# Group 4's attention output turned by the DMA crossbar instead of TensorE, and the block that reads it begun by halves of 256 tokens

## The chip, the core and the metric

The kernel runs on one core of one Trainium2 chip. The time is the device time of that core in microseconds (us). A core has five engines that work side by side, each through its own instructions in its own order: TensorE (PE in the profile) multiplies matrices, and its weight loads are shown apart as PEld; VectorE (DVE), ScalarE (ACT) and GpSimd (POOL) work element by element; SyncE (SP) does nothing here but issue DMA transfers. An engine whose next instruction waits does not go on to the one behind it.

## The reference

Two layers follow each other. The first is attention in which a query sees the first 4 keys ("sinks") and the 128 latest ones; there are 4 batches, 8 heads, 768 positions and a head size of 64. The second is a feed-forward block on the 3072 tokens of 512 features that come out of it.

```python
scores = scale * np.matmul(q, k.transpose(0, 1, 3, 2))
keep = (pos[None, :] < n_sink) | ((rel >= 0) & (rel < window))
a = softmax(np.where(keep, scores, -1e9))
x = np.matmul(a, v).transpose(0, 2, 1, 3).reshape(B * S, H * D)
g, val = x @ w_gate, x @ w_val          # 512 -> 1536, twice
out = (g * sigmoid(g) * val) @ w_out    # 1536 -> 512
```

## The kernel before, in words

**Groups and blocks.** The attention works on 12 groups of 256 tokens, three to a batch (groups 0 to 2 are batch 0, and so on; `c` is a group's place in its batch). The feed-forward works on blocks of tokens: blocks 0, 1 and 2 have 256 tokens each (groups 0, 1, 2), blocks 3 to 6 have 512 (groups 3 and 4, 5 and 6, 7 and 8, 9 and 10), and block 7 has 256 (group 11).

**The steps of a group.** From group 4 on, a group goes through these:
- `NV(g)`: GpSimd issues four loads of k and q into the tile `nat` (line 111) and two of v into `va` (line 122). All groups from 4 on share one buffer for `nat`, so the loads of group g+1 wait until group g's `nat` has been read.
- `xbar(g)`: SP issues four DMA transposes from `nat` to kT and qT (line 255), in the order k, q of the first 128 tokens, k, q of the last 128. "The crossbar" is this kind of DMA.
- `step_S(g, 0)` and `(g, 1)`: the scores of heads 0 to 3 and 4 to 7 (matmuls of line 288), ScalarE's exponential (295), VectorE's mask (300). `step_K` does the sinks' scores (line 316).
- `step_PV(g, j, hh)`: probabilities times v for 128 tokens j and half of the heads hh (lines 331 and 351), then VectorE's reciprocal and product into `xn` (359, 365). A group has four, in the order hh 0 with j 0 and 1, then hh 1 with j 0 and 1.
- `step_X(g, j)`: turns `xn` of 128 tokens into `xT`, features on the partitions. For groups in the list `PEX` this is four TensorE transposes (line 392) and a VectorE copy (line 399); for the others SP issues one DMA transpose (line 387). It is called X(g, j) below.

**The feed-forward.** A gate unit computes 512 columns: four matmuls of 512 columns for the gate (tile `pg`, line 413), ScalarE's tanh (433), four matmuls for the value (`pv`), and two VectorE instructions that make `ht` (441, then 447 or 443). For a block of 256 tokens one unit takes two of the twelve slices of 128 features, in eight matmuls of 256 columns each. A down unit computes 128 tokens of the output in twelve matmuls (`pd`, line 488), a ScalarE copy (493) and a DMA to the output (496).

**The order.** It is written out by hand: `manual_schedule` keeps it as the program issues it. `weave` runs a list of units and puts the attention's steps into them: into a gate unit between the gate's and the value's matmuls, into a down unit evenly between its twelve matmuls. The first weave has 24 units, 0 to 23; units 18 to 23 are the down units of blocks 0, 1 and 2, and it holds the steps of groups 2, 3 and 4 and the first loads of 5, 6 and 7. The second weave has the twelve gate units and four down units of block 3 and holds groups 5 and 6; scores of group 6 (`step_S(6, 0)`) stand in its unit 6. The third does the same for block 4 and groups 7 and 8, the fourth for block 5 and groups 9 and 10.

Three orders matter around the change. SP issues xbar(5), the output of unit 19, X(3, 0), X(3, 1), the outputs of units 20, 21 and 22, xbar(6), the output of unit 23, xbar(7), X(5, 0), X(5, 1). GpSimd issues NV(5), then `behind(3, 255)`, NV(6), NV(7), `behind(4, 511)`, NV(8). `behind(tb, t)` (line 521) copies one element of column t of xT of block tb, so it holds GpSimd, and with it the loads behind it, until that column has been turned. TensorE does the score matmuls of group 6 when it comes to them; nothing behind them passes them.

PSUM tiles all come from one pool of eight banks that are used in turn, so a step can wait for the reader of the tile eight allocations back.

Of the kernel before, what the change touches and what calls it, by code (L numbers as in the profile page):

```python
# [10 lines left out]
ALU = mybir.AluOpType  # L11
# [3 lines left out]
def kernel(  # L15
# [12 lines left out]
    nc = tc.nc  # L28
# [13 lines left out]
    SIZES = [256, 256, 256, 512, 512, 512, 512, 256]  # L42
    assert sum(SIZES) == NTOK and NG == 12
    OFF = [sum(SIZES[:i]) for i in range(len(SIZES))]
    PEX = (0, 1, 2, 4)

    VS = 72
    FCH = [2] * 6
# [29 lines left out]
    def bank(shape, dtype, name):  # L78
        return psum.tile(shape, dtype, tag="b", name=name)
# [123 lines left out]
    kTs, qTs, es_t, e_t, xns, xTs = {}, {}, {}, {}, {}, {}  # L203
# [168 lines left out]
    def dense(t, c, n):  # L372
        return t[:, 0:c * n].rearrange("p (c n) -> p c n", c=c)

    def step_X(g, j, evict="v"):
        t0 = g * 256 + j * P
        tb = max(i for i in range(len(SIZES)) if OFF[i] <= t0)
        off = t0 - OFF[tb]
        if tb == 0 and off == 0:
            xTs["01"] = xtp.tile([P, DMC, 512], BF16, tag="xT", name="xT")  # L380
            xTs[0], xTs[1] = (xTs["01"][:, :, 256 * i:256 * (i + 1)] for i in range(2))
        elif tb > 1 and off == 0:
            xTs[tb] = dense(xtp.tile([P, DMC * 512], BF16, tag="xT", name="xT"),
                            DMC, SIZES[tb])
        if g not in PEX:
            def sp():
                nc.sync.dma_start_transpose(xTs[tb][:, :, off:off + P], xns[g, j])
            later.append(sp)
            return
        pt = bank([P, DMC, P], BF16, "px")  # L390
        for i in range(DMC):
            nc.tensor.transpose(pt[:, i], xns[g, j][:, i * P:(i + 1) * P], ident)  # L392

        if evict == "a":
            nc.scalar.copy(out=xTs[tb][:, :, off:off + P], in_=pt)
            return

        def dve():
            nc.vector.tensor_copy(out=xTs[tb][:, :, off:off + P], in_=pt)
        if evict == "now":  # L400
            dve()
        else:
            later.append(dve)

    hts = {}

    def project(ws, tb, f, name):
        n = xTs[tb].shape[2]
        ps = bank([P, 512], FP32, name)
        for i in range(512 // n):  # L410
            fi, fo = FOF[f + i]
            for c in range(DMC):
                nc.tensor.matmul(  # L413
                    ps[:, i * n:(i + 1) * n], ws[fi][:, c, fo * P:(fo + 1) * P],
                    xTs[tb][:, c], start=(c == 0), stop=(c == DMC - 1))
        return ps

    def gate_a(tb, f):
        new_h(tb)
        return tanh(project(wgs, tb, f, "pg"))  # L420

    def new_h(tb):
        if tb not in hts:
            n = SIZES[tb]
            t = hpool.tile([P, DFC * 512], BF16, tag="ht", name="ht")
            hts[tb] = dense(t, DFC, n)
            if tb == 0:
                hts["01"] = t.rearrange("p (b c n) -> p b c n", b=2, c=DFC)
                hts[1] = t[:, DFC * n:2 * DFC * n].rearrange("p (c n) -> p c n", c=DFC)

    def tanh(pg):
        th = tpool.tile([P, 512], FP32, tag="th", name="th")
        nc.scalar.activation(th, pg, AF.Tanh, scale=0.5)  # L433
        return pg, th

    def gate_b(tb, f, pg, th):
        gate_v(tb, f, pg, th, project(wvs, tb, f, "pv"))

    def gate_v(tb, f, pg, th, pv):
        u = upool.tile([P, 512], BF16, tag="u", name="u")  # L440
        nc.vector.scalar_tensor_tensor(u, th, 1.0, pg, op0=ALU.add, op1=ALU.mult)  # L441
        if tb == "01":
            nc.vector.tensor_tensor(
                hts[tb][:, :, f], *(x.rearrange("p (b n) -> p b n", b=2) for x in (u, pv)),
                op=ALU.mult)
            return
        nc.vector.tensor_tensor(  # L447
            hts[tb][:, f:f + 512 // SIZES[tb]].rearrange("p a n -> p (a n)"), u, pv,
            op=ALU.mult)

    def gate(tb, f, attn):
        a = gate_a(tb, f)
        for step in attn:
            step()
        gate_b(tb, f, *a)
        flush()
# [3 lines left out]
    def gate_held(tb, f, attn):  # L460

        held.append(A(gate_v, tb, f, *gate_a(tb, f), project(wvs, tb, f, "pv")))

    def gate_first(tb, f, attn):

        for j, hh, norm in ((0, 0, "a"), (1, 0, "v"), (0, 1, "v"), (1, 1, "a")):
            step_PV(1, j, hh, norm)
            flush()
        a = gate_a(tb, f)
        step_X(1, 0, "now")  # L470
        step_X(1, 1, "now")
        held.pop()()
        gate_b(tb, f, *a)
# [24 lines left out]
    def gates(tb):  # L498
        return [(gate, tb, f) for f in range(0, DFC, 512 // SIZES[tb])]

    def downs(tb):
        return [(down, tb, t) for t in range(SIZES[tb] // P)]

    def A(fn, *a):
        return lambda: fn(*a)
# [4 lines left out]
    def Ss(g):  # L510
        return [A(step_S, g, p2) for p2 in range(2)]

    def PVs(g):
        return [A(step_PV, g, j, hh) for hh in range(2) for j in range(2)]

    def Xs(g):
        return [A(step_X, g, j) for j in range(2)]
# [5 lines left out]
    def K(g):  # L523
        return A(step_K, g)

    def weave(us, slots):
        assert all(i < len(us) for i in slots)
        for i, (fn, tb, x) in enumerate(us):
            fn(tb, x, slots.get(i, []))

    def slots(*pairs):
        sl = {}
        for at, steps in pairs:
            for i, step in zip(at if isinstance(at, tuple) else (at,) * len(steps),
                               steps):
                sl.setdefault(i, []).append(step)
        return sl
# [114 lines left out]
    def L(*fs):  # L652
        def f():
            for x in fs:
                x()
        return f

    def NV(g):
        return L(A(load_nat, g), A(load_v, g))
# [7 lines left out]
        (15, [A(xbar, 4)]), (15, [NV(5)]), (19, [A(xbar, 5)]),  # L667
        (23, [A(xbar, 6)]), (23, [NV(7)]),
        ((17, 18), Ss(3)), (18, [A(step_ks, 1)]), (18, [A(step_vsb, 1)]),
        ((19, 19, 19, 20), PVs(3)), (20, [*Xs(3), flush, A(behind, 3, 255), NV(6)]),  # L670
        (19, [L(Ss(4)[0], K(4))]), (20, Ss(4)[1:]),
        ((21, 21, 22, 22), PVs(4)), (22, Xs(4))))

    def pair(ga, gb, sh=0):
        s = sh
        return [((s, s + 2), Ss(ga)), (s, [K(ga)]),
                ((s + 4, s + 5, s + 6, s + 7), PVs(ga)),
                ((s + 6, s + 8), Ss(gb)), ((s + 8, s + 9), Xs(ga)), (s + 6, [K(gb)]),
                ((12, 12, 13, 13) if s else (10, 10, 11, 12), PVs(gb)),
                ((14, 14) if s else (12, 13), Xs(gb))]  # L680

    weave(gates(3) + downs(3), slots(
        (2, [A(xbar, 7)]), (15, [A(step_ks, 2), A(step_vsb, 2)]), *pair(5, 6),
        (13, [flush, A(behind, 4, 511), NV(8)]),
        (15, [A(xbar, 8)]), (15, [NV(9)])))
# [43 lines left out]
```

## Time and profile before

| | |
|---|---|
| median of 7 runs | 238.46 us (237.86 to 238.8) |
| profiled execution, its own time | 238.63 us |
| span of the profile | 236.9 us |
| granted TensorE clock, mean | 0.999 |
| busy: TensorE, VectorE, ScalarE, GpSimd | 97%, 67%, 48%, 32% of the span |
| first weave's down units | 55.2 to 75.3 us on TensorE |
| block 3's gate units | 75.3 to 100.6 us |

The page's first part gives the busy time of each engine, and its fourth part follows the chain of work that ended last. The timeline lists an engine's instructions with their start and length in us, equal neighbours merged; SPq rows are the moments at which SP issues a DMA, POOL rows of kind DMA_DIRECT2D those in which GpSimd writes a load's descriptors. A bracket at the end of a row tells how long the engine had been idle and what ended that. The trace also records when each DMA's completion reached its semaphore.

### The profile page before, as it was taken

What the parts mean: (1) busy time and instruction counts of PE and PEld (TensorE: products, weight loads), DVE (VectorE), ACT (ScalarE), POOL (GpSimd) and SP (SyncE); (2) the same over time, 40 slices, a digit from 0 to 9 for tenths busy, and PEclk for the clock granted to TensorE, in tenths of its full rate; (3) what the DMA queues carried; (4) which work ended last, traced back from release to release, by engine and by line L of the source; (5) the groups of instructions that cost most, each with busy time, mean ns of one, the idle gap of its engine ahead of it and who ended that gap; (6) DMA issues with size and microseconds to landing.
All of it is one profiled execution on the core that took longest, in us unless ns stands there. A gap on an engine that the chain in (4) does not pass through costs nothing.

```text
span 236.9 us, 4855 instructions
## 1 busy us (share of the span) xinstructions
PE 228.9 (97%) x1858; PEld 125.8 (53%) x1885; DVE 158.8 (67%) x335; ACT 113.5 (48%) x235; POOL 74.7 (32%) x99
## 2 busy tenths in 40 slices
PE   8899999999999999999999999999999999999994
PEld 4568645795554444544445444444544445488443
DVE  5897888768652888950898980698970598877000
ACT  4794485467453836412846522655622653333221
POOL 8996865713505344005353440080000000000000
PEclk9999999999999999999999999999999999999999
DMA  8999999994999999927989996599314100200132
GB/s 133 160 184 177 181 200 205 160 146 76 157 176 180 127 133 131 118 49 152 150 123 136 119 142 159 134 86 118 66 24 144 56 3 0 44 3 0 55 124 91
DMA packets 107655, 27.36 MB, mean 116 GB/s; under 512 B 94704, under 2 KB 104688, under 8 KB 107632
## 3 DMA queue, kind: packets, MB, share of 16 engines
q0 software_dynamic: 76640, 13.90, 77.2%
q1 hardware_dynamic: 30448, 12.89, 27.4%
q8 instruction: 15, 0.25, 0.4%
q10 hardware_dynamic: 544, 0.26, 0.4%
q14 instruction: 8, 0.07, 0.1%
HBM read 28.34 MB, written 6.29 MB: 146 GB/s over the span
## 4 chain that ended last, share of the span: by engine, by line
PE 89%; DVE 2%; DMA 2%; POOL 2%; issue 2%; ACT 1%; POOLq 0%; DVEq 0%; ACTq 0%
PE pv L413 26%; PE pd L488 26%; PE pg L413 25%; PE s L288 4%; PE o L351 4%; DMA rows<-in_q_dram 2%; DVE xn L365 1%; PE o L331 1%; PE pn L241 1%; POOL rows L100 1%; POOL x L186 1%; PE pk L316 1%; ACT th L433 1%; PE px L392 1%; DVE rcp L359 0%
## 5 line engine op out<-in xcount | busy, mean ns | idle before, releaser
L441 DVE SCALAR_TENSOR_TENSOR u<-th,pg 128x512 bf16<-128x512 f32 x72 | 49.2, 683 | 38.2 <-ACT th L433 38.2
L413 PE MATMUL pg<-xT,wg 128*128 128x512 bf16 (+1 forms) x345 | 73.4, 340 | 0.7
L433 ACT ACTIVATE th<-pg 128x512 f32<-128x512 f32 x72 | 43.4, 603 | 62.9 <-PE pg L413 59.2
L413 PE MATMUL pv<-xT,wv 128*128 128x512 bf16 (+1 forms) x341 | 72.8, 339 | 0.6 <-ACT e L295 0.2
L488 PE MATMUL pd<-wo,ht 128*128 128x512 bf16 (+2 forms) x291 | 64.7, 370 | 0.6 <-issue 0.2
L447 DVE TENSOR_TENSOR ht<-u,pv 128x512 bf16<-128x512 bf16 x64 | 44.0, 688 | 9.6 <-PE pv L413 2.9
L413 PEld LDWEIGHTS <-wg 128*128 128x128 bf16 x352 | 34.3, 98 | 28.4 <-issue 0.4
L295 ACT ACTIVATE e<-s 128x512 bf16<-128x512 f32 (+1 forms) x88 | 42.8, 579 | 3.9 <-PE s L288 3.7
L488 PEld LDWEIGHTS <-ht 128*128 128x128 bf16 x300 | 27.8, 98 | 29.9 <-issue 0.3
L413 PEld LDWEIGHTS <-wv 128*128 128x128 bf16 x352 | 31.4, 98 | 20.9 <-issue 1.7
L493 ACT ACTIVATE ot<-pd 128x512 f32<-128x512 f32 (+1 forms) x24 | 14.3, 596 | 47.2 <-PE pd L488 43.2
L111 POOL DMA_DIRECT2D nat<-in_k_dram x20 | 17.7, 888 | 47.5 <-DMA qT<-nat 43.8
L300 DVE TENSOR_TENSOR e<-e,mask 128x1024 bf16<-128x1024 bf16 (+1 forms) x44 | 27.0, 650 | 3.8 <-ACT e L295 3.8
L122 POOL DMA_DIRECT2D va<-in_v_dram x24 | 21.5, 921 | 4.2 <-DMA wo<-in_moe_w_out_dram 2.5
L365 DVE TENSOR_TENSOR xn<-o,rcp 128x256 bf16<-128x256 f32 x44 | 18.7, 425 | 1.5
L351 PEld LDWEIGHTS <-e 128*128 128x128 bf16 x352 | 15.0, 98 | 7.8 <-issue 0.2
L111 POOL DMA_DIRECT2D nat<-in_q_dram x20 | 17.7, 899 | 1.2 <-DMA wv<-in_moe_w_val_dram 0.5
L351 PE MATMUL o<-va,e 128*128 128x65 bf16 x352 | 17.0, 194 | 0.1
L288 PE MATMUL s<-qT,kT 64*128 64x128 bf16 (+1 forms) x240 | 12.9, 237 | 0.0
L288 PEld LDWEIGHTS <-kT 64*128 64x128 bf16 x240 | 7.7, 94 | 7.5 <-issue 6.6
L495 DVE TENSOR_SCALAR ot<-pd 128x128 f32<-128x128 f32 x1 | 0.3, 292 | 14.3 <-PE pd L488 14.3
L359 DVE RECIPROCAL rcp<-o 128x4 f32<-128x4 f32 x48 | 8.4, 176 | 1.2 <-PE o L351 1.1
(72 smaller groups left out, 93.2 us busy)
## 6 DMA issues: line engine op xcount, KB each, us to landing
out_dram<-ot SPq DMA_DIRECT2D x23, 256.0 KB
va<-in_v_dram POOLq DMA_DIRECT2D x24, 128.0 KB, 6.5
nat<-in_k_dram POOLq DMA_DIRECT2D x20, 128.0 KB, 4.1
nat<-in_q_dram POOLq DMA_DIRECT2D x20, 128.0 KB, 5.9
wg<-in_moe_w_gate_dram POOLq DMA_DIRECT2D x6, 256.0 KB, 8.0
wv<-in_moe_w_val_dram POOLq DMA_DIRECT2D x6, 256.0 KB, 8.3
wo<-in_moe_w_out_dram POOLq DMA_DIRECT2D x4, 384.0 KB, 11.2
st<-in_q_dram ACTq DMA_DIRECT2D x2, 128.0 KB
```

What stands on the lines that cost most here:

```text
L111: nc.gpsimd.dma_start(x[:, i, j].rearrange("p (h d) -> p h d", d=D), src[b, :, t0:t0 + P].rearrange("h p d -> p h d"))
L122: nc.gpsimd.dma_start(va[:, j, :, 0:D], v[b, :, t0:t0 + P].rearrange("h p d -> p h d"))
L288: nc.tensor.matmul(pss[2 * pp + h][:, col:col + n], kTs[b][r, p, kk:kk + P], qTs[b][r, p, qq:qq + n], start=True, stop=True)
L295: nc.scalar.activation(e_t[g][:, h0 + h, lo:512], pss[2 * pp + h][:, lo:512], AF.Exp, scale=scale)
L300: nc.vector.tensor_tensor(e, e, m[:, :, lo:512].broadcast_to([P, 2, 512 - lo]), op=ALU.mult)
L351: nc.tensor.matmul(o, l, r, start=(c == 0 and i == 0), stop=(i == len(mms) - 1), skip_group_check=True)
L365: nc.vector.tensor_tensor(xn, po[:, :, 0:D], rcp.broadcast_to([P, 4, D]), op=ALU.mult)
L413: nc.tensor.matmul(ps[:, i * n:(i + 1) * n], ws[fi][:, c, fo * P:(fo + 1) * P], xTs[tb][:, c], start=(c == 0), stop=(c == DMC - 1))
L433: nc.scalar.activation(th, pg, AF.Tanh, scale=0.5)
L441: nc.vector.scalar_tensor_tensor(u, th, 1.0, pg, op0=ALU.add, op1=ALU.mult)
L447: nc.vector.tensor_tensor(hts[tb][:, f:f + 512 // SIZES[tb]].rearrange("p a n -> p (a n)"), u, pv, op=ALU.mult)
L488: nc.tensor.matmul(po, hts[tb][:, f, ts * P:(ts + 1) * P], wos[f // n][:, f % n, lo:hi], start=(f == 0), stop=(f == DFC - 1))
```

## The change

Group 4 leaves `PEX`, so X(4, 0) and X(4, 1) become DMA transposes on SP. The first two gate units of block 3, which took feature slices 0 and 1 over all 512 tokens, become one unit for slices 0 and 1 of the first 256 tokens (group 3) and one for the same slices of the last 256 (group 4). The second of them alone, of the two, needs group 4. In the first weave the steps of units 20 to 22 are redistributed: X(4, 0) goes to unit 21 behind the third of group 4's four PV steps, X(4, 1) to unit 22 behind the fourth. `behind` and NV(6) move from unit 20 to unit 22, and `behind` now waits for column 511 of block 3's xT, that is for X(4, 1), where it waited for column 255.

SP's order becomes: xbar(5), output 19, X(3, 0), X(3, 1), output 20, X(4, 0), output 21, X(4, 1), output 22, xbar(6), output 23, and on as before.

```diff
-    PEX = (0, 1, 2, 4)
+    PEX = (0, 1, 2)
...
+            if tb == 3:
+                for i in range(2):
+                    xTs[tb, i] = xTs[tb][:, :, 256 * i:256 * (i + 1)]
...
     def gate_a(tb, f):
-        new_h(tb)
+        new_h(tb[0] if isinstance(tb, tuple) else tb)
...
+        if isinstance(tb, tuple):
+            nc.vector.tensor_tensor(
+                hts[tb[0]][:, f:f + 2, 256 * tb[1]:256 * (tb[1] + 1)],
+                *(x.rearrange("p (a n) -> p a n", a=2) for x in (u, pv)), op=ALU.mult)
+            return
...
-        ((19, 19, 19, 20), PVs(3)), (20, [*Xs(3), flush, A(behind, 3, 255), NV(6)]),
+        ((19, 19, 19, 20), PVs(3)), (20, Xs(3)),
         (19, [L(Ss(4)[0], K(4))]), (20, Ss(4)[1:]),
-        ((21, 21, 22, 22), PVs(4)), (22, Xs(4))))
+        ((21, 21, 21, 22), PVs(4)), (21, Xs(4)[:1]),
+        (22, [Xs(4)[1], flush, A(behind, 3, 511), NV(6)])))
...
-    weave(gates(3) + downs(3), slots(
+    weave([(gate, (3, i), 0) for i in range(2)] + gates(3)[2:] + downs(3), slots(
```

## The prediction

> **What bounds the kernel now.** I read the page first, for the engine that is never idle, then the timelines of TensorE, SP and GpSimd around units 20 to 30, which the change touches.
>
> ```profile
> span 236.9 us, 4855 instructions
> ...
> PE 228.9 (97%) x1858; PEld 125.8 (53%) x1885; DVE 158.8 (67%) x335; ACT 113.5 (48%) x235; POOL 74.7 (32%) x99
> ...
> PE 89%; DVE 2%; DMA 2%; POOL 2%; issue 2%; ACT 1%; POOLq 0%; DVEq 0%; ACTq 0%
> ```
>
> TensorE is busy 97% of the span and makes 89% of the chain that ended last: matmul time that goes is won, and a stall of TensorE is lost. Its timeline, where group 4 is turned and where group 6's scores come:
>
> ```profile
> 71.14 0.39 PE L392 MATMUL px<-ident,xn 128*128 128x128 bf16 x4
> 71.36 0.59 PE L488 MATMUL pd<-wo,ht 128*128 128x512 bf16 x2
> 71.80 0.39 PE L392 MATMUL px<-ident,xn 128*128 128x128 bf16 x4
> 72.02 3.40 PE L488 MATMUL pd<-wo,ht 128*128 128x512 bf16 x14
> 75.26 1.03 PE L413 MATMUL pg<-xT,wg 128*128 128x512 bf16 x4
> ...
> 89.17 0.50 PE L288 MATMUL s<-qT,kT 64*128 64x256 bf16 x8
> 89.78 1.04 PE L413 MATMUL pv<-xT,wv 128*128 128x512 bf16 x4
> ```
>
> From start to start, four transposes take 71.14 to 71.36, 0.22 us; block 3 begins at 75.26; group 6's scores at 89.17. SP's queue, then GpSimd's:
>
> ```profile
> 69.75 1.22 SPq L387 DMA_TRANSPOSE xT<-xn  x1
> 71.06 2.81 SPq L496 DMA_DIRECT2D out_dram<-ot  x3
> 77.21 1.19 SPq L255 DMA_TRANSPOSE kT<-nat  x1
> 79.65 1.19 SPq L255 DMA_TRANSPOSE qT<-nat  x1
> 80.94 1.22 SPq L255 DMA_TRANSPOSE kT<-nat  x1
> 82.54 1.19 SPq L255 DMA_TRANSPOSE qT<-nat  x1
> ...
> 105.22 0.49 SPq L496 DMA_DIRECT2D out_dram<-ot  x1
> 105.82 1.23 SPq L387 DMA_TRANSPOSE xT<-xn  x1
> ```
>
> ```profile
> 72.96 0.18 POOL L521 CAST warmed<-xT 1x1 f32<-1x1 bf16 x1 [10.65 <-DMA xT<-xn]
> 73.73 1.77 POOL L111 DMA_DIRECT2D nat<-in_k_dram  x2 [0.60 <-issue]
> ...
> 86.05 1.76 POOL L111 DMA_DIRECT2D nat<-in_k_dram  x2 [7.04 <-DMA qT<-nat]
> ...
> 108.35 0.17 POOL L521 CAST warmed<-xT 1x1 f32<-1x1 bf16 x1 [17.04 <-DMA xT<-xn]
> ```
>
> GpSimd waits for X(3, 1), issued at 69.75, until 72.96; starts group 6's loads at 73.73; and at 86.05 has seen group 6 turned. So group 6 is ready 3.1 us ahead of its scores. That margin is what the change spends.
>
> **Part 1: eight transposes leave TensorE.** 8 x 0.055 (0.22 / 4) = 0.44 us, on the path: matmuls stand right before and after them. VectorE's two copies of xT, 0.42 us each, end at 72.65, and VectorE then sits idle 4.23 us for block 3's first tanh: worth nothing.
>
> **Part 2: halves.** Units 24 and 25 have eight matmuls of 256 columns where four of 512 stood, in four places. The chain has both forms: eight of 256 in block 7 take 0.87 us, four of 512 take 0.86. Cost 4 x 0.01 = 0.04 us. ScalarE's tanh is the same 128x512; VectorE's strided product (line 443) takes 688 ns, as does the plain one (447). Sum so far: -0.44 + 0.04 = -0.40 us.
>
> **Part 3: PV steps move up.** Group 4's third PV moves from unit 22 (69.58) to unit 21, about 68.1. It needs the last mask of step_S(4, 1), which VectorE ends at 67.27 + 0.69 = 67.96; that score step moves up by one matmul (0.22), so about 67.74. Cover 0.1 to 0.35 us, price nothing; without the cover at most 0.2.
>
> **Part 4: two transposes on SP.** An output takes 0.6 us of SP to the next issue (105.22 to 105.82; up to 0.8 behind a transpose), a transpose 1.31 (69.75 to 71.06). So output 20 at 71.06, X(4, 0) about 71.8, output 21 at 73.1 (was 71.86), X(4, 1) at 73.7, output 22 at 75.0 (was 73.54). Both xn are ready earlier, 69.6 and 70.8 by the PV times and 0.6 us of VectorE a step. The outputs delay nobody: ot has four buffers, and the next output tile after unit 23 is written at 103.59. xbar(6), queued behind, waits for data until 77.21 even in the old order. X(4, 1) in the new order follows a transpose and an output, as X(6, 1) did: issued 105.82, GpSimd released 108.35, 2.53 us. By X(3, 1) it is 3.21. So X(4, 1) is there at 76.2, at worst 76.9. Unit 24 starts at 74.82 and needs only X(3), there at 72.96. Unit 24 took 2.61 us (75.26 to 77.86) and takes 2.63, so unit 25 starts at 77.4. Cover 0.5 to 1.2 us, price nothing.
>
> **Part 5: the loads held.** This adds the wait that matters. Behind GpSimd's `behind` are NV(6), NV(7) and `behind(4, 511)`; for NV(6) wait xbar(6) on SP, the scores of group 6 on TensorE, and NV(7). From the release to the first load 0.77 us (72.96 to 73.73), 1.06 in the other case (108.35 to 109.41). So the loads start at 77.0, bounds 76.9 and 78.0, instead of 73.73. From the first load to group 6 turned and seen by GpSimd: 73.73 to 86.05, 12.32; group 8 the same way 11.87 (109.41 to 121.28), group 9 12.50 (121.28 to 133.78). In the trace's completion records the last q transpose landed at 85.49, so GpSimd's step adds 0.56 and landing takes 11.76; by the same records groups 5 and 7 take 12.08 and 11.83, and group 11, the far row, 13.62. I take group 6's own 11.76, since its loads meet the same neighbours (output 22 at the start, its own four transposes): 77.0 + 11.76 = 88.75. Ends: 76.9 + 11.31 (group 8) = 88.2, and 78.0 + 13.62 = 91.6.
>
> Need: 89.17 - 0.40 = 88.77. There is a little more: the pv matmuls behind the scores wait at 89.78 for a PSUM bank that VectorE's xn (89.30, 0.42 long) frees, while the scores are done at 89.61. That chain (tanh at 87.06, u, ht, reciprocal, xn) moves with TensorE, so scores that start up to 0.17 late, 88.94, cost nothing. With a weight load (0.09) after landing they start at 88.85. **Stall: nothing at the likely value, 0 to 2.7 us at the ends.** The whole forecast hangs on 0.1 us here.
>
> A rule speaks against this part. The Trainium skill, "SBUF — State Buffer", section "SBUF: two separate sides", says that a load issued by GpSimd can starve, since GpSimd can't write descriptors while VectorE holds their shared port in its fast modes. The loads move from 73.5 to 79.2, where VectorE is busy 1.82 us of 5.70, to 76.9 to 82.5, and from 78 to 82 it is busy 3.80 of 4.00. The trace doesn't show the price: six loads keep GpSimd 5.27 us there and 5.26 from 86.0 to 91.5, where VectorE is busy 4.45 of 5.50. By the rule each load could wait out one 0.69 us VectorE instruction, 4.1 us in all as an estimate from that page, and the time would be some 242; by the rows it is nothing, and I go by the rows.
>
> **Part 6: what follows later.** NV(7) starts at 89.3 instead of 86.05, xbar(7)'s last issue goes from 95.28 to 98.5, X(5, 0) and X(5, 1) from 96.61 and 97.90 to 99.9 and 101.2. X(6, 0), at 103.14, finds SP free again. Group 7's scores are needed at 112.12, block 4's input at 111.16: 7 us of cover and more. Nothing.
>
> **The sum.** -0.44 + 0.04 + 0 = -0.40 us. The profiled execution took 238.63, of which 1.7 us lie outside the span and do not change: 238.23. It lay 0.17 above the median, so the median becomes 238.06, say 238.1.
>
> **Rivals.** *Group 6 late (slower).* TensorE stands at step_S(6, 0) in unit 30. Below a landing of 88.85 it costs nothing; from 89.25 it has eaten the gain; from 89.7 the kernel is over 0.2% slower. Group 11's 13.62 from 77.0 gives 90.6: stall 1.75, time +1.35, 239.8. For it: one of five groups took that long, and X(3, 0) had one of its sixteen completions 1.6 us behind the rest, which in X(4, 1) would hold the loads as long and end near there too (and cost unit 25 up to 0.4). Against it: four of five lie between 11.3 and 12.1. *The gain is swallowed.* TensorE, held at the semaphore until 88.75, has an empty queue behind it; if it refills slowly, or if landing is 0.3 later, the gain is 0 to 0.1: 238.4. *More than the matmuls goes.* The 0.17 us wait at 89.78 shrinks as well, and the halves cost nothing: -0.44 - 0.17 = -0.61, 237.85. Nothing in the chain asks for it, since that wait hangs on tanh and VectorE.
>
> **Chances.** 0.2% is 0.48 us, about what a measurement of this kernel tells from no change. The main case has 55%, its own range 237.9 to 238.5; as its -0.40 is close to the bound, I give 15 of the 55 to "faster". Swallowed 13%, all "same". More 10%, faster. Group 6 late 22%, 20 of them slower, the other 2 within the bound. That makes faster 25%, same 55%, slower 20%. The range runs from 237.8, the third rival, to 239.3, which takes in the milder half of the late cases and leaves out about 1 in 10 above.
>
> **What would show it.** Right: no line 392 between 66 and 75 us; unit 24 at 74.8; X(4, 1) issued near 73.7; GpSimd's cast near 76.2 and its first load near 77.0; step_S(6, 0) at 88.8 with no wait of TensorE on a DMA before it. Wrong: a gap of TensorE before unit 25 or before line 288 near 89 us, ended by DMA xT or qT; six GpSimd loads that take over 5.4 us; scores of group 6 past 89.7.

## The result and the profile after

The changed kernel takes 240.73 us in the median of 13 runs (238.94 to 242.91), the kernel before 238.44 in 32 (237.82 to 239.73). The ratio is 1.0084, interval 1.0066 to 1.0101: about 2.0 us slower, where 238.1 and a range up to 239.3 were forecast. The ratio leaves out the executions furthest above the fastest, so it is a little under that of the medians. The spread matters as much as the median: 4 us against 2 before. The profiled execution, 238.94 us, is the fastest of the 13, so its profile shows the loss at its smallest.

The changed kernel has some lines more, so its line numbers are higher: the gate's matmuls stand in 416 (413 before), the transposes of xT in 390 (387) on SP and 395 (392) on TensorE, the outputs in 504 (496), `behind` in 529 (521). The first part and the fourth of the page of after, to lay beside the three lines of before:

```profile
span 237.2 us, 4878 instructions
...
PE 228.6 (96%) x1867; PEld 127.5 (54%) x1893; DVE 157.7 (66%) x333; ACT 113.7 (48%) x235; POOL 74.7 (31%) x99
...
PE 60%; DMA 20%; POOL 8%; issue 8%; SPq 2%; ACT 0%; DVE 0%; POOLq 0%
```

TensorE is about as busy as before, but the chain that ended last no longer runs along it: its share fell from 89% to 60%, and DMA and GpSimd together rose from 4% to 28%. TensorE's timeline, with start and length in us and, in brackets, idle time and what ended it, tells where the two chains meet:

```profile
74.37 1.04 PE L416 MATMUL pg<-xT,wg 128*128 128x256 bf16 x8
...
76.99 1.04 PE L416 MATMUL pg<-xT,wg 128*128 128x256 bf16 x8
...
87.98 0.41 PE L351 MATMUL o<-va,e 128*128 128x65 bf16 x8
89.81 0.51 PE L288 MATMUL s<-qT,kT 64*128 64x256 bf16 x8 [1.42 <-DMA qT<-nat]
90.25 1.04 PE L416 MATMUL pv<-xT,wv 128*128 128x512 bf16 x4
```

The eight transposes are gone, unit 24 starts at 74.37 (forecast 74.82), unit 25 at 76.99 without a wait, and TensorE comes to group 6's scores at 88.39 (88.77) and stands there 1.42 us, until the q transposes of group 6 have landed. SP and GpSimd in the same execution:

```profile
73.85 1.24 SPq L390 DMA_TRANSPOSE xT<-xn  x1
75.19 0.53 SPq L504 DMA_DIRECT2D out_dram<-ot  x1
80.79 1.20 SPq L255 DMA_TRANSPOSE kT<-nat  x1
...
85.46 1.22 SPq L255 DMA_TRANSPOSE qT<-nat  x1
```

```profile
76.42 0.18 POOL L529 CAST warmed<-xT 1x1 f32<-1x1 bf16 x1 [13.83 <-DMA xT<-xn]
77.16 1.77 POOL L111 DMA_DIRECT2D nat<-in_k_dram  x2 [0.57 <-issue]
...
90.54 1.76 POOL L111 DMA_DIRECT2D nat<-in_k_dram  x2 [8.11 <-DMA qT<-nat]
```

X(4, 1) is issued at 73.85 (forecast 73.7), GpSimd is released at 76.42 (76.2), the loads start at 77.16 (77.0). Up to here the forecast of the DMA side held in this execution. Then GpSimd sees group 6 turned at 90.54, not 89.3.

### The profile page after: what moved, and what is told of

Read it like the earlier page. It is cut to its first block, busy times and chain, and to the rows that moved or that the text cites. A ratio compares the mean times of both kernels' runs of the same rounds, so it can differ in the third digit from the quotient of the medians.

```text
span 237.2 us, 4878 instructions
## 1 busy us (share of the span) xinstructions
PE 228.6 (96%) x1867; PEld 127.5 (54%) x1893; DVE 157.7 (66%) x333; ACT 113.7 (48%) x235; POOL 74.7 (31%) x99
## 4 chain that ended last, share of the span: by engine, by line
PE 60%; DMA 20%; POOL 8%; issue 8%; SPq 2%; ACT 0%; DVE 0%; POOLq 0%
PE pd L496 20%; PE pv L416 18%; PE pg L416 17%; DMA wv<-in_moe_w_val_dram 7%; DMA wo<-in_moe_w_out_dram 5%; DMA nat<-in_q_dram 5%; DMA qT<-nat 3%; POOL nat L111 3%; PE o L351 3%; PE s L288 2%; POOL va L122 2%; SPq L255 2%; POOL rows L100 1%; POOL x L186 1%; POOL wo L140 1%
## 5 line engine op out<-in xcount | busy, mean ns | idle before, releaser
L416 PEld LDWEIGHTS <-wg 128*128 128x128 bf16 x360 | 35.1, 98 | 27.9 <-issue 0.4
L455 DVE TENSOR_TENSOR ht<-u,pv 128x512 bf16<-128x512 bf16 x62 | 42.7, 688 | 10.7 <-PE pv L416 3.8
L416 PEld LDWEIGHTS <-wv 128*128 128x128 bf16 x360 | 32.1, 98 | 20.2 <-issue 1.9
```

The lines of the kernel that those rows point to most:

```text
L416: nc.tensor.matmul(ps[:, i * n:(i + 1) * n], ws[fi][:, c, fo * P:(fo + 1) * P], xTs[tb][:, c], start=(c == 0), stop=(c == DMC - 1))
L455: nc.vector.tensor_tensor(hts[tb][:, f:f + 512 // SIZES[tb]].rearrange("p a n -> p (a n)"), u, pv, op=ALU.mult)
```

## The experiments

My first theory after the result was H: it is the hold that costs, because group 6 is turned too late. Its rival was X: the crossbar turn of group 4, whose lateness would show in front of unit 25.

**The changed kernel again**, for a profile of another execution.

> The changed kernel itself, profiled once more, because its one profile (238.94 us) is its fastest execution and the median is 240.73. Theory H (the held loads): group 6 is turned later in a typical execution than in that profile, where TensorE stood 1.42 us before the scores of group 6; in a profile near 240.7 that one wait is 3 to 3.5 us and unit 25 starts without a wait. Rival X (the crossbar turn of group 4): the typical execution loses its time in front of unit 25, because X(4, 1) lands after 77.4 us, and the wait at the scores stays near 1.4.

The median was 240.66 us of 5 runs, ratio 1.0066 (1.0044 to 1.0089). The profiled execution was the slowest, 243.97. Its TensorE timeline has three waits:

```profile
75.94 1.03 PE L416 MATMUL pg<-xT,wg 128*128 128x256 bf16 x8 [1.03 <-DMA xT<-xn]
...
79.86 1.03 PE L416 MATMUL pg<-xT,wg 128*128 128x256 bf16 x8 [1.12 <-ACT es L320]
...
93.08 0.51 PE L288 MATMUL s<-qT,kT 64*128 64x256 bf16 x8 [1.83 <-DMA qT<-nat]
```

Unit 24 waited for X(3, 1), unit 25 for X(4, 1) (the profile names ScalarE; the trace's completion records put the landing of X(4, 1) at 79.72), and the scores for group 6, landed at 92.99. So neither H nor X alone: everything on the DMA side was about 3 us later than in the first profile, while TensorE came to unit 24 at 74.91, no later than before the change (75.26). These waits also cost more than themselves, as the stretches of 4 us show (busy time of each engine, then the granted clock of TensorE):

```profile
90.00:94.00 4.00, 2.17 (x24) 1.21 (x23) 2.22 (x5) 1.16 (x3) 0.20 (x1) 1.00 1.12 118
94.00:98.00 4.00, 4.00 (x19) 1.76 (x18) 2.83 (x6) 1.67 (x4) 4.00 (x5) 0.57 1.15 73
```

After the wait at the scores the clock was at half for 3.41 us, 1.7 us of matmul time lost on top.

**The hold taken back.**

```diff
-        (22, [Xs(4)[1], flush, A(behind, 3, 511), NV(6)])))
+        (22, [Xs(4)[1], flush, A(behind, 3, 255), NV(6)])))
```

> The changed kernel with its wait back on column 255, that is for X(3, 1), so that group 6's loads start at about 73 us as before; group 4 stays on the crossbar and the halves stay. H: the scores of group 6 wait for nothing (turned at about 85.5, needed at 88.8) and the gain of 0.40 is there: 238.0 us, 237.8 to 238.4, with a spread as small as before. If the loads, now in flight beside X(4, 1), make that land late, unit 25 stalls: X(4, 1) past 77.4, and 0.4 us of delay gives the whole gain back. X: no better than the changed kernel, 240 or more, with the wait in front of unit 25.

Measured 243.15 us in the median of 6 runs, ratio 1.0135 (1.0087 to 1.0182): the gain does not come back. The median is above that of the changed kernel, but the intervals just overlap. SP and TensorE in its profile:

```profile
75.30 1.23 SPq L390 DMA_TRANSPOSE xT<-xn  x1
76.62 0.54 SPq L504 DMA_DIRECT2D out_dram<-ot  x1
```

```profile
80.38 1.03 PE L416 MATMUL pg<-xT,wg 128*128 128x256 bf16 x8 [2.92 <-DMA xT<-xn]
```

X(4, 1), issued at 75.30, lands at 80.25: 4.95 us with group 6's loads in flight, against 2.48 to 2.51 in the seven profiles in which the loads are held. Unit 25 waits 2.92 us for it; group 6 is early (87.08) and its scores wait for nothing. In this profile the hold is shown to do what it is for. The case that the expectation kept open for H came true, and the loss moved from the scores to unit 25.

**The halves alone**, with group 4 on TensorE and everything else as before:

```diff
-    weave(gates(3) + downs(3), slots(
+    weave([(gate, (3, i), 0) for i in range(2)] + gates(3)[2:] + downs(3), slots(
```

> The kernel before with the halves alone: units 24 and 25 by halves of 256 tokens, group 4 turned on TensorE, loads released by X(3, 1), steps of units 20 to 22 as before. H and X both: 0.04 us more than before, 238.5 us, within 0.1%. A third cause, that the halves themselves cost (sixteen more matmuls and weight loads, strided writes of VectorE), would show as 239 or more.

238.6 us, ratio 0.9998 (0.9984 to 1.0011). The halves are as cheap as forecast. One of the 12 runs took 242.77 us at a mean clock of 0.985; its cause stays open.

**The hold alone**, in the kernel before, with the release tied to TensorE's progress instead of to a DMA: `hold` copies one element of unit 23's output tile, which ScalarE writes when that unit's matmuls are done. The last line below stands in the second weave.

```diff
+        nc.gpsimd.tensor_copy(out=warmed[0:1], in_=ots[2, 1][0:1, 0:1])
...
-        (23, [A(xbar, 6)]), (23, [NV(7)]),
...
-        ((19, 19, 19, 20), PVs(3)), (20, [*Xs(3), flush, A(behind, 3, 255), NV(6)]),
+        ((19, 19, 19, 20), PVs(3)), (20, Xs(3)),
...
+        (0, [hold, NV(6), A(xbar, 6), NV(7)]),
```

> The kernel before with the held loads alone: group 4 turned on TensorE, no halves, but group 6's loads wait for the output tile of unit 23, written at about 76.1 us, where X(4, 1) lands at 76.4 in the changed kernel; the transposes of group 6 follow behind them on SP. H: when the scores of group 6 can start is set by the loads, not by TensorE, so the time is that of the changed kernel: 240 to 241 us, with its wide spread, and a wait of TensorE on a DMA before line 288 near 89 us. X: 238.5, as before.

238.78 us, ratio 1.0008 (0.9995 to 1.0021): H falls as it was put. Here GpSimd's timeline and TensorE's read:

```profile
75.62 0.18 POOL L502 COPY warmed<-ot 1x1 f32<-1x1 f32 x1 [13.72 <-DMA out_dram<-ot]
76.39 1.77 POOL L111 DMA_DIRECT2D nat<-in_k_dram  x2 [0.59 <-DMA out_dram<-ot]
```

```profile
89.20 0.51 PE L288 MATMUL s<-qT,kT 64*128 64x256 bf16 x8 [0.51 <-DVE xn L365]
```

(The bracket of the copy names a DMA, but ScalarE's write of the tile ends at 75.56.) The loads start at 76.39, 2.7 us later than in the profile of before; group 6 lands at 89.07, the scores start at 89.20, and hardly anything is lost. A hold of that length just fits the margin. It is shorter than any hold of the changed kernel, whose loads start at 77.02 to 80.52, so this experiment does not tell a hold that is too long from one that ends with a DMA chain whose time differs from run to run. The second is theory C, the chain. The completion records of all profiles of kernels with group 4 on the crossbar and loads held bear on it (us; "turned" is the last landing of group 6's transposes):

| profile | X(3, 1) landed | X(4, 1) landed | loads start | turned | load to turned |
|---|---|---|---|---|---|
| before, for comparison | 72.91 | | 73.73 | 85.49 | 11.76 |
| forecast | 72.9 | 76.2 | 77.0 | 88.75 | 11.76 |
| after | 73.25 | 76.36 | 77.16 | 89.72 | 12.56 |
| after, again | 75.81 | 79.72 | 80.52 | 92.99 | 12.47 |
| scores later | 74.39 | 78.24 | 79.04 | 91.46 | 12.42 |
| four slices | 72.56 | 76.22 | 77.02 | 89.60 | 12.58 |
| both | 73.82 | 77.72 | 78.52 | 90.53 | 12.01 |
| no halves | 74.83 | 78.74 | 79.54 | 90.79 | 11.25 |
| both, again | 73.44 | 77.33 | 78.12 | 90.31 | 12.19 |

The seven profiles from "after" on are of kernels with the same program up to unit 23, so the 3 us between the earliest and the latest X(3, 1) are not the doing of the edits between them. Unit 24 starts between 74.17 and 75.94 in all of them but "no halves", where it waits for X(4, 1). The last five rows come from the experiments below, the first three of which take away the two needs, unit 25's for X(4, 1) and the scores' for group 6, one by one and together. Their rivals: the wait at the scores is all; unit 25's wait is all; or S, the crossbar's traffic slows the machine wherever the waits show.

**The scores of group 6 two units later:**

```diff
-                ((s + 6, s + 8), Ss(gb)), ((s + 8, s + 9), Xs(ga)), (s + 6, [K(gb)]),
+                ((s + 6 + late, s + 8 + late // 2), Ss(gb)), ((s + 8, s + 9), Xs(ga)), (s + 6, [K(gb)]),
...
-        (2, [A(xbar, 7)]), (15, [A(step_ks, 2), A(step_vsb, 2)]), *pair(5, 6),
+        (2, [A(xbar, 7)]), (15, [A(step_ks, 2), A(step_vsb, 2)]), *pair(5, 6, 0, 2),
```

> The changed kernel with group 6's scores two gate units later (units 8 and 9 instead of 6 and 8). The held loads alone cost nothing, so theory C (the chain) replaces H: X(4, 1) lands 76.4 to 79.7 us, because it is the last link of SP's queue behind the loads and transposes of group 5, whose time differs from run to run, and from its landing everything is counted: 0.8 to the first load, 12.5 to group 6 turned. What is lost is then the landing of group 6 past 88.9 us, 2.6 us in the median. C: with the scores needed at about 92.6 that wait is gone, and what is left is unit 25's wait for X(4, 1), 0 to 2.3 us: 238.3 to 239.3. If the wait at the scores is all, 238.1. Rival S (the crossbar's traffic slows TensorE or the other transfers themselves, wherever the waits show): 240 or more.

238.58 us of 11 runs (237.86 to 240.67), ratio 1.0011 (0.9992 to 1.0030). The wait at the scores is gone, and nearly all of the loss with it; what its profile still has is a wait in front of unit 25 (X(4, 1) landed at 78.24):

```profile
78.38 1.03 PE L416 MATMUL pg<-xT,wg 128*128 128x256 bf16 x8 [1.07 <-ACT es L320]
```

**Four slices by halves**, so that X(4, 1) is needed one unit later, with the scores where the change has them:

```diff
-    weave([(gate, (3, i), 0) for i in range(2)] + gates(3)[2:] + downs(3), slots(
+    weave([(gate, (3, i), f) for i in range(2) for f in (0, 2)] + gates(3)[4:] + downs(3), slots(
```

> The changed kernel with four slices by halves instead of two, so that X(4, 1) is needed by unit 26, 2.6 us later, and group 6's scores where they are. C: the wait at the scores comes last and takes up what unit 25 no longer waits, so nothing is won: 240 to 241.2. If unit 25's wait were the loss, 238.2.

239.53 us of 12 runs, ratio 1.0072 (1.0042 to 1.0102). The median is under the expected range, but the ratio's interval overlaps those of the changed kernel (1.0084, 1.0066), so they are not told apart. More slack at unit 25 alone does not bring the gain. Four of the 12 runs have a mean clock of 0.993 and took 241.75 to 242.09; the eight others took 238.76 to 240.29, with a middle of 239.4, where the changed kernel's ten runs with the full clock took 238.94 to 241.91, with a middle of 240.5. If that difference is real, C, by which nothing is won here, does not explain it. The wait stands where C has it:

```profile
89.69 0.51 PE L288 MATMUL s<-qT,kT 64*128 64x256 bf16 x8 [0.98 <-DMA qT<-nat]
```

**Both edits together.**

> The changed kernel with both: four slices by halves, scores of group 6 two units later. C: TensorE waits for neither, and the 0.36 us (eight transposes of 0.055, eight places of 0.01) are there: 238.1, faster than the kernel before by 0.1 to 0.2%, with a spread as small. S: 240 or more.

238.12 us of 12 runs (237.56 to 238.79), ratio 0.9989 (0.9977 to 1.0001). In its profile TensorE waits for no DMA between 70 and 100 us, though X(4, 1) landed at 77.72 and group 6 at 90.53, both too late for the changed kernel:

```profile
77.39 1.04 PE L416 MATMUL pg<-xT,wg 128*128 128x256 bf16 x8
...
92.46 0.50 PE L288 MATMUL s<-qT,kT 64*128 64x256 bf16 x8
```

S falls: the same transfers cost nothing once nobody waits for them.

**The change without the halves**, unit 24 over all 512 tokens:

```diff
-    weave([(gate, (3, i), 0) for i in range(2)] + gates(3)[2:] + downs(3), slots(
+    weave(gates(3) + downs(3), slots(
```

> The changed kernel without the halves: group 4 on the crossbar, loads held until X(4, 1), block 3's units over all 512 tokens. Unit 24 then waits for X(4, 1), needed at 74.8 instead of 77.4. C: the wait at the scores comes last here too and is counted from the same landing, so the time is nearly that of the changed kernel, 240.3 to 241.3. If unit 25's wait were the loss, 2.6 us more than it: 243.

241.59 us of 6 runs, ratio 1.0125 (1.0082 to 1.0168). The median lies above C's figure, 240.3 to 241.3, and the runs fall into two sets. Three with the full clock took 240.08, 240.42 and 240.73, at its lower end and like the changed kernel. Three with a mean clock of 0.993 took 242.46 to 243.74. The profile is of one of these: unit 24 waits 3.46 us, and the clock halves behind it (0.75 is the mean of the stretch):

```profile
78.83 1.02 PE L416 MATMUL pg<-xT,wg 128*128 128x512 bf16 x4 [3.46 <-issue]
```

```profile
78.00:82.00 4.00, 3.17 (x27) 1.35 (x28) 0.69 (x1) 2.11 (x5) 2.63 (x4) 0.75 0.52 91
```

So C's sum misses a term: a long wait can cost a stretch at half clock besides.

**Is the version with both faster than the kernel before?** It was run again, beside a control with the same order and group 4 turned on TensorE.

> The kernel with four slices by halves and the later scores once more, since its interval (ratio 0.9977 to 1.0001) just reached the kernel before. C: 0.36 us under it again, ratio about 0.9985.

> The same order, four slices by halves and the scores of group 6 later, but group 4 turned on TensorE and the loads released by X(3, 1), as before the change. C: the gain of that kernel comes from the eight transposes alone, so here it is gone and the eight places of halves cost 0.08: 238.5, ratio 1.000 to 1.001. If the later scores or the halves brought the gain, ratio 0.998 to 0.999 here too.

The version with both: 238.22 us of 12 runs against 238.53, ratio 0.9998 (0.9979 to 1.0018); this time its spread was 237.31 to 239.65. The control: 238.52, ratio 1.0004 (0.9992 to 1.0016), as C expects. The two medians of the version lie 0.35 and 0.31 us under those of the kernel before, close to the 0.36 of the transposes less the halves, but both intervals include 1: that it beats the kernel before is not shown. That it beats the changed kernel is.

## Why the prediction was wrong

**What bounds the kernel** was read rightly: TensorE's time was the path, and the change put another chain there.

**Parts 1 and 2** hold in the profiles. No transpose on TensorE stands between 66 and 75 us, units 24 and 25 begin 2.62 us apart (2.63 forecast), and the halves alone measure 0.9998. With both needs moved out of the way the median falls by 0.31 to 0.35, where these two parts give 0.36 with four slices; the intervals don't tell that gain from nothing. **Part 3** holds: no wait in units 20 to 22.

**Part 4 is the first step that failed.** Its mechanism is right: X(4, 1) lands 3.1 to 3.9 us behind X(3, 1) in the seven profiles, forecast 3.3, and 2.5 us behind its issue. What it is added to is wrong. SP's times came from the one profile of before and were taken as constants: X(3, 1) issued at 69.75, there at 72.9. In the seven profiles of the table SP issues X(3, 1) at 69.45 to 73.36 and it is there at 72.56 to 75.81 (74.83 without the slowest execution); X(4, 1), forecast to be issued at 73.7, is issued at 73.72 to 77.22. So "there at 76.2, at worst 76.9" became 76.2 to 79.7, with a middle of 77.7, and "cover 0.5 to 1.2 us, price nothing", counted from the forecast 77.4, was 1.2 at best and less than nothing in four of the seven. My worst case varied the latency of one DMA and left its starting time fixed.

**Part 5 is the second.** I saw that "the whole forecast hangs on 0.1 us", and took 11.76 us from load to turned, group 6's own figure, where the other groups in the same trace have 11.31, 11.83, 11.95, 12.08 and 13.62. Measured: 12.0 to 12.6 in six of seven, 11.25 in one. Its other term inherits part 4's error. Turned was forecast at 88.75 and came at 89.6 to 93.0, always past the 88.85 from which it costs. So the stall that the sum put at nothing was about 2.4 us: the 2.0 that the kernel lost and the 0.40 that it should have won. The margins of before, 2.3 us at unit 24 and 3.1 at group 6's scores, looked like room to spend; the profiles speak for their being what kept the variation off TensorE. In the four with group 4 on TensorE X(3, 1) lands at 72.91 to 74.03, and the one of before is the earliest; unit 24 starts at 74.71 to 75.26 without a wait, so the margin there was 0.7 to 2.3 us. The hold alone shows only that a hold of 2.7 us, which ends with a unit of TensorE, cost 0.14 us in the median, which is not told from nothing.

**A price not in the sum**: the half clock after long waits. Of the changed kernel's 13 runs three have a mean clock of 0.993, what one stretch of 3.41 us at half clock makes, at 240.29, 242.61 and 242.91; the kernel before has none under 0.998 in the runs listed with these experiments. That waits cause it is seen in two profiles and not tested; the run of 242.77 us with the halves alone had a low clock too.

**The rule** on GpSimd and VectorE was rightly set aside. In the profile after, from 77.1 to 82.5 us, VectorE is busy 5.00 us of 5.40 and GpSimd's six loads take 5.27, as before.

**The rivals.** "Group 6 late" is what happened, at its place, but only half by its mechanism: it took 13.62 us from load to turned, where 11.25 to 12.58 were measured, and the loads at their forecast 77.0, where they started up to 3.5 us later. Its price, 239.8, was short by 1 us. I gave it 22%, since I asked how often one group takes 13.6 us from load to turned, and not how far all the links before it vary together. Even the middle of the six values in that one trace, 11.9 in place of 11.76, puts group 6 at 88.9, past the point from which it costs.

**What stays open** is why X(3, 1) varies by 3 us. In the second profile of the changed kernel the k and q loads of group 5 landed at 67.39 instead of 64.75, and its transposes at 72.52 instead of 68.91. I have not separated the causes; one candidate stands below. Whether the variation alone or also its middle, later than forecast, made the loss is not separated either.

## What to carry to other kernels

Before a margin is spent, it is to be compared with how much both sides of it vary from run to run, and one profile doesn't tell that: its spread has to come from several profiles, or from equal steps elsewhere in the trace, taken at their middle and not at their best. A release tied to the end of a DMA chain carries that chain's variation into all that follows; tied to the progress of the bounding engine, a somewhat shorter delay was nearly free. When work leaves the bounding engine for a queue, whatever needs its result, and whatever the queue does next, has to be moved later by the spread and not only by the mean: here two units for the scores and one for the second half turned +0.84% into about nothing or a little less.

## What the runs showed of the hardware

**Transposes beside loads.** A DMA transpose of 128x512 bf16 between SBUF tiles held SP about 1.2 us. Group 4's two landed 2.4 to 2.6 us after their issue in the seven profiles with held loads, where no loads of k, q or v were in flight; X(3, 1), issued close behind X(3, 0), took 2.4 to 3.7 us in the twelve profiles. With loads of 128 KB issued by GpSimd in flight X(4, 1) took 4.95 us (the experiment without the hold), and the first transpose of group 6, behind its own loads, 5.5 to 7.3 us.

**The clock.** After the waits described, TensorE was at half clock for 3.41 us in two profiles. The drops came at 94.46 and 80.03 us, 26.0 and 22.0 times 3.413 us after the full clock began (at 5.71 and 4.94). The stretch of 3.413 us before the drop contains 1.83 us without a matmul in the one (91.25 to 93.08), 2.22 in the other (to 78.83). A wait of 2.92 us in the kernel without the hold was followed by no drop: counted in the same way it lies across two stretches, with 1.08 us in the first and 1.84 in the second. So the idle time in a stretch does not by itself tell whether the clock drops. The Trainium skill, "TensorE: Matmul & The Clock Gate", section "Part 1: The HAM clock gate (the "warmup" mystery)", gives the window as 3413 ns, running freely, which these two drops agree with. It says that the clock falls after at least one idle window; here the clock fell after windows idle for 54% and 65%, so the measurement differs.

**Instruction fetches.** The page of before lists a queue "q8 instruction" with 15 packets of 16 KB; its packet records put one at 69.4 to 70.5 us in all twelve profiles, 0.9 to 1.5 us long, near the issues of the transposes of group 3, and the next at 84.0 to 93.9. That these packets fetch instructions is read from the queue's name. In the profile of before, 15 of the 16 completions of X(3, 0) came by 70.98 us and the last at 72.58; in the profile after, 15 of those of the last load of v for group 6 came by 86.76 and the last at 88.62, behind the packet at 86.38. That the packet held up one DMA engine is an inference; no run moved these packets.
